# Four column tiles of 32 output rows for each TensorE matmul but the logits, in a gated mix of infini-attention and GEGLU

## The chip, the cores and the metric

The kernel runs on one core of a Trainium2 chip. The metric is the device time in microseconds, the median over runs. All of TensorE (PE), VectorE (DVE), ScalarE (ACT), GpSimd (POOL) and SyncE (SP, which issues the DMAs) take part; each works through its own instructions in program order, and semaphores tie them together.

## The reference

The input x is 2048 rows of 512 (bf16). Two branches read it, and a gate per row mixes them.

```python
g = sigmoid((x * gate_w).sum(-1))                     # one gate per row
out = g * a(x) + (1 - g) * b(x)

# b: GEGLU, inner width 1792
b = (gelu_tanh(x @ w_gate) * (x @ w_up)) @ w_down

# a: 32 heads of 16; the rows in N = 4 segments of L = 512
phi = lambda t: where(t > 0, t + 1, exp(t))
gb = sigmoid(beta)                                    # one number per head
for s in range(4):
    qs, ks, vs = ...                                  # of this segment, per head
    a_dot = softmax(qs @ ks.T / 4 + causal) @ vs
    a_mem = (phi(qs) @ M) / (phi(qs) @ z + 1e-6)      # memory of the segments before
    outs.append(gb * a_mem + (1 - gb) * a_dot)
    M += phi(ks).T @ vs                               # 16 x 16 per head
    z += phi(ks).sum(rows)
a = concat(outs) @ wo
```

## The kernel before, in words

**Layout.** x is kept transposed in `xT`, features on the 128 partitions: four chunks `fc` of 128 features, 2048 columns of rows. Heads come in four chunks `c` of eight (8 x 16 = 128 partitions); in a chunk the heads lie in four pairs `j` of 32 partitions, an even head (`e` = 0) and an odd one. `pr` is a pair of chunks. A segment's 512 rows are four tiles `kt` (or `qt`) of 128.

**Three forms of matmul.** A TensorE matmul takes a stationary operand (loaded ahead by its own instruction, LDWEIGHTS) and streams the columns of a moving one.
- Full: stationary 128 x 128, output on 128 partitions. So work the projections q and k, gate and up (`mm_x`, L320; the first segment's k at L406), v (L422), down (`down`, L834) and output projection (`proj_o`, L839), the memory's denominators (L780) and numerators (L810), the memory update M (L739), and the small ones at the start: `warm` (L371), the transposes of x (L391) and `bps` (L506).
- Row tiles: the logits (`logit_slot`, L574). Four heads at a time, each on its own 16 or 32 partitions of contraction, `tile_position=(32*j, 0)`, each with 128 output partitions.
- Column tiles: softmax times v (`pv_group`, L626) and the gate rows (`gate_rows`, L441). Four matmuls with a stationary operand of 128 x 32, `tile_position=(0, 32*j)`, each writing its own 32 output partitions.

**Memory.** For each pair of chunks of a segment, phi(k) is made by ACT (exp), DVE and POOL (L690 to L701), transposed by DMA (L730), and multiplied with v: `m_update` runs, for each of two chunks and four tiles `kt`, one full matmul with 8 x 17 = 136 moving columns (16 values and a one per head, `VW` = 17). Of its 128 x 136 result only the blocks in which key head and value head agree are wanted. DVE adds the result to `Macc` (L752, L754), and multiplies the value columns with a block mask that also holds the factor of beta (`bdeb`) into `Mbd` (L761), and the ones' columns with a mask into `zbd` (L764). The next segment reads `Mbd` and `zbd`.

**Softmax.** A slot (20 per segment, five per chunk) holds four heads' logits in two PSUM tiles of 128 x 1024; ACT takes the exponential of each (L597), POOL masks it (L606), then come the pv groups, one for the even and one for the odd heads of a chunk. DVE transposes their result (L644), divides it, adds the memory's share and transposes it back into `xT` (L654 to L670), whose columns are free by then.

**PSUM.** The logits, gate pairs and some output tiles share three tiles of two banks (ring `lg`); everything else shares two of one bank (ring `gen`).

**Order.** Each piece of work is a named task; the string `ORDER` (L31 to L102) lists them all by hand, and `Sched.run` emits them in that order, engine by engine. In it PE's small groups (logits `lg`, `pv`, memory) alternate with full ones (`up`, `dn`, `q`, `k`, `v`), about one or two of these between two logit slots. The gates and a part of `up` come first, in the first 75 us; attention runs from there to 250 us; the last segments' down and output projections end the kernel.

The first lines that the change touches, in `mm_x`:

```python
for fc in range(FC):
    nc.tensor.matmul(t, lhsT=W[:, fc, c0:c0 + P], rhs=xT[:, fc, s * L:(s + 1) * L],
                     start=(fc == 0), stop=(fc == FC - 1))
```

Of the kernel before, what the change touches and what calls it, by code (L numbers as in the profile page):

```python
# [23 lines left out]
NCH = H // 8  # L24
HS = DFF // P
# [4 lines left out]
MM = 216  # L30
# [119 lines left out]
def kernel(  # L150
# [39 lines left out]
    def ctile(name, shape, dtype=BF):  # L190
        return cp.tile(shape, dtype, name=name, tag=name)
# [30 lines left out]
    zbd = ctile("zbd", [P, NCH * (P + 2)])  # L222
    bdeb = ctile("bdeb", [P, NCH, 8, DH])
    Mbd = ctile("Mbd", [P, NCH, 8, DH])
    Macc = ctile("Macc", [P, NCH, 8, VW], F32)
    G2 = ctile("G2", [P, NSEG, QB], F32)
    omz = ctile("omz", [P, NSEG, KT], F32)
    omg = ctile("omg", [P, NCH], F32)
# [77 lines left out]
    def evac(engs, g, box, fn, kind="copy", deps=(), alloc=(), frees=(), ring="gen"):  # L306
        return add("e" + g.name, engs, lambda e: fn(e, box["t"]), kind=kind,
                   deps=[g] + list(deps), alloc=alloc, frees=[(ring, g)] + list(frees))

    QK = {}  # L310
    EVQK = {}
    first_ev = {}
# [4 lines left out]

    def mm_x(t, W, c0, s):
        for fc in range(FC):
            nc.tensor.matmul(t, lhsT=W[:, fc, c0:c0 + P], rhs=xT[:, fc, s * L:(s + 1) * L],  # L320
                             start=(fc == 0), stop=(fc == FC - 1))

    def kfree(s, pr):
        k = first_ev[("k", s, pr)]
# [39 lines left out]
    def first_k():  # L364

        tl = {}

        def f_warm(_):
            t = lgtile("warm")
            for i in range(NWARM):  # L370
                nc.tensor.matmul(t[:, 0, :], lhsT=warm[:, 0:P], rhs=warm,  # L371
                                 start=True, stop=True)
# [13 lines left out]
        xe = []  # L386
        prev = op
        for fc in range(FC):
            def f_t(_, fc=fc):
                for kt in range(KT):  # L390
                    nc.tensor.matmul(tl["x", fc][:, kt * P:(kt + 1) * P],  # L391
                                     lhsT=xn[:, kt, fc * P:(fc + 1) * P], rhs=ident,
                                     start=True, stop=True)
            prev = add(f"xt{fc}", "PE", f_t, cost=416, deps=[prev, a_xn])
            xe.append(add(f"ext{fc}", "ACT" if fc % 2 else "DVE",
                          lambda e, fc=fc: copy(e, xT[:, fc, 0:L], tl["x", fc]), kind="copy",
                          deps=[prev], frees=[(("lg", 0), op) if fc < 2
                                              else (("gen", fc - 2), op)]))
        a_x[0] = xe[-1]
        TAB["wdn"] = add("wdn", "SP", lambda _: load_w(nc.sync, wdn, B_w_down), deps=[prev],  # L400
                         kind="wdn")
        last = None
        for fc in range(FC):
            def fn(_, fc=fc):
                for c in range(NCH):
                    nc.tensor.matmul(tl["k", c // 2][:, c % 2, :],  # L406
                                     lhsT=wk[:, fc, c * P:(c + 1) * P], rhs=xT[:, fc, 0:L],
                                     start=(fc == 0), stop=(fc == FC - 1))
            last = add(f"k0f{fc}", "PE", fn, cost=4 * MM, deps=[last, xe[fc], a_wk])
            read_x[0].append(last)  # L410
        for c in range(NCH):
            first_ev[("k", 0, c // 2)] = op
            EVQK[("k", 0, c)] = add(f"ek0.{c}", ["DVE", "ACT"],
                                    lambda e, c=c: copy(e, QK[("k", 0, c // 2)][:, c % 2, :],
                                                        tl["k", c // 2][:, c % 2, :]),
                                    kind="copy", deps=[last], frees=[(("lg", 1 + c // 2), op)])
            odd_copy(0, c, EVQK[("k", 0, c)])

    def v_group(s, kt, engs):
        def mms(t):  # L420
            for fc in range(FC):
                nc.tensor.matmul(t[:, :], lhsT=xT[:, fc, s * L + kt * P:s * L + (kt + 1) * P],  # L422
                                 rhs=wv[:, fc, :], start=(fc == 0), stop=(fc == FC - 1))
# [12 lines left out]
    def gate_rows():  # L436

        def mms(t):
            for fc in range(FC):
                for s in range(NSEG):  # L440
# [4 lines left out]
        g, box = group("", "gz", 4 * MM, mms, a_x + [TAB["gwB"]], mode="col")  # L445
        tl = {}

        def f_tt(e, t):
# [54 lines left out]
    TAB["gwB"] = add("gwB", "DVE", f_gwB, kind="gwB", deps=[a_gw])  # L503

    def f_bps(t):
        nc.tensor.matmul(t[:, 0:NCH], lhsT=hot8[:, :, :].rearrange("p a b -> p (a b)"),  # L506
                         rhs=beta8[:, :], start=True, stop=True)

    def f_omg(e):
        nc.vector.tensor_scalar(out=omg[:, :], in0=tb[:, :], scalar1=-0.5, scalar2=0.5,  # L510
# [104 lines left out]
    def pv_group(s, c, e):  # L615
# [19 lines left out]
            deps.append(PVT[s][-1])  # L635
        def mk():
            TT[(s, c)] = rtile("T", [P, 2, QB, 32], F32)
        g, box = group(f"{s}.{c}{'eo'[e]}", "pv", 546, mms, deps, mode="col", also=("T", mk) if e == 0 else None,
                       frees=[("pT", XT_[(g0 + w, h)]) for w in slots for h in range(2)])
        PVT[s].append(g)  # L640
        key = (s, c)
# [92 lines left out]
    def m_update(s, pr):  # L734
        def mms(t):
            for i in range(2):
                c = 2 * pr + i
                for kt in range(KT):
                    nc.tensor.matmul(t[:, i * 8 * VW:(i + 1) * 8 * VW],  # L739
                                     lhsT=PKt[(s, pr)][:, i, kt, :],  # L740
                                     rhs=vz[s % 2][:, kt, 8 * c * VW:8 * (c + 1) * VW],
                                     start=(kt == 0), stop=(kt == KT - 1))
        g, box = group(f"{s}.{pr}", "M", 8 * 66, mms,
                       [PKD[(s, pr)]] + [EVV[(s, kt)] for kt in range(KT)]
                       + ([TAB[("mbd", s - 1)], TAB[("zbd", s - 1)]] if s else []),
                       frees=[("pk", PKD[(s, pr)])])
# [2 lines left out]
        def f_acc(e, t):  # L749
            dst = Macc[:, 2 * pr:2 * pr + 2, :, :].rearrange("p c h w -> p (c h w)")  # L750
            if s == 0:
                nc.vector.tensor_copy(dst, t[:, 0:16 * VW])  # L752
            else:
                nc.vector.tensor_add(dst, t[:, 0:16 * VW], dst)  # L754
        acc = evac("DVE", g, box, f_acc, kind="acc")
        TAB[("acc", s, pr)] = acc
        if pr == 0:
            return

        def f_mbd(_):  # L760
            nc.vector.tensor_mul(Mbd[:, :, :, :], Macc[:, :, :, 0:DH], bdeb[:, :, :, :])  # L761

        def f_zbd(_):
            nc.vector.tensor_mul(  # L764
                zbd[:, :].rearrange("p (c n) -> p c n", c=NCH)[:, :, 0:P]
                .rearrange("p c (j m) -> p c j m", j=4)[:, :, :, 0:2],
                Macc[:, :, :, DH].rearrange("p c (j e) -> p c j e", j=4),
                bd[:, :, 0].rearrange("p (j e) -> p j e", j=4)[:, None, :, :]
                .to_broadcast((P, NCH, 4, 2)))
        deps = [TAB[("acc", s, 0)], acc, t_eb] + [TAB[("num", s, c)] for c in range(NCH) if s]  # L770
# [4 lines left out]
    def mem_den(s):  # L775
        bx = {}

        def mms(t):
            for c in range(NCH):
                nc.tensor.matmul(t[:, :], lhsT=zbd[:, c * P:(c + 1) * P],  # L780
                                 rhs=PQ[(s, c // 2)][:, c % 2, :],
                                 start=(c == 0), stop=(c == NCH - 1))
# [24 lines left out]

    def mem_num(s, c):
        def mms(t):
            nc.tensor.matmul(t[:, :], lhsT=Mbd[:, c, :, :].rearrange("p h d -> p (h d)"),  # L810
                             rhs=PQ[(s, c // 2)][:, c % 2, :], start=True, stop=True)
# [19 lines left out]

    def down(t, s, qt, lo, hi, stop):
        for hs in range(lo, hi):
            nc.tensor.matmul(t[:, :], lhsT=G[:, s, hs, qt * P:(qt + 1) * P], rhs=wdn[:, hs, :],  # L834
                             start=(hs == 0), stop=stop and (hs == HS - 1))

    def proj_o(t, s, qt, cs, first):
        for c in cs:
            nc.tensor.matmul(t, lhsT=xT[:, c, s * L + qt * P:s * L + (qt + 1) * P],  # L839
                             rhs=wo[:, c, :], start=first and c == 0, stop=(c == NCH - 1))  # L840

    def store(s, qt, osb):
        q0 = s * L + qt * P
# [112 lines left out]
```

## Time and profile before

| | |
|---|---|
| time, median of 3 runs | 283.71 us (283.68 to 283.9) |
| the profiled execution's own time | 283.82 us |
| its span in the profile | 282.1 us |
| PE busy | 271.1 us, 96%, 2280 matmuls recorded |
| weight loads (PEld) | 118.4 us, 2320 recorded |
| ACT busy | 204.2 us, 72% |
| DVE busy | 174.6 us, 62% |
| POOL busy | 125.9 us, 45% |
| granted PE clock | full in all 40 slices |
| code loads (q8) | 18 of 16 KB |

The span runs from the first to the last instruction in the profile; the execution's own time holds the start and the end around it. Shares are of the span. A matmul's record is longer than the time until the next one may start, since matmuls overlap: a full one of 512 columns shows 380 ns, and the next starts 216 ns later. So what a matmul costs PE is read from start to start, and a busy PE need not stream. A few matmul records are missing from the trace (2280 of 2320).

### The profile page before, as it was taken

The numbers are of one execution on the slowest core, as the hardware profiler recorded it, in microseconds if no ns is written. First come the engines' busy times: TensorE is split into PE (matmuls) and PEld (weight loads), VectorE is DVE, ScalarE is ACT, GpSimd is POOL, SyncE is SP. The second block draws the span as 40 slices with busy tenths as digits, with TensorE's granted clock in tenths as the row PEclk, the third lists the DMA queues.
The fourth block names the chain that finished last, engine by engine and source line by source line (L and its number), as shares of the span: only waits on it lengthen the run. The fifth ranks groups of instructions, "written<-read, shape, count | busy, mean of one in ns | idle before, by whom it ended". The sixth has DMA issues, their size and how long they took to land.

```text
span 282.1 us, 5660 instructions
## 1 busy us (share of the span) xinstructions
PE 271.1 (96%) x2280; PEld 118.4 (42%) x2320; DVE 174.6 (62%) x324; ACT 204.2 (72%) x223; POOL 125.9 (45%) x220
## 2 busy tenths in 40 slices
PE   8999999999999999999899999999999999999994
PEld 4444444444444443444334444433444444344441
DVE  2100002510787878999969659989698877857721
ACT  3555654326689989999999999999999999950000
POOL 8000000060066686495575858584547657650000
PEclk9999999999999999999999999999999999999999
DMA  7973970000002211100001101000002000000011
GB/s 233 347 129 75 344 251 2 0 0 2 1 19 46 15 30 28 21 0 2 2 0 21 37 3 38 2 21 1 2 0 58 21 19 21 2 21 0 21 56 57
DMA packets 22019, 13.74 MB, mean 49 GB/s; under 512 B 14056, under 2 KB 20968, under 8 KB 21992
## 3 DMA queue, kind: packets, MB, share of 16 engines
q1 hardware_dynamic: 21448, 12.85, 16.8%
q10 hardware_dynamic: 544, 0.52, 0.5%
q8 instruction: 18, 0.29, 0.4%
q14 instruction: 9, 0.07, 0.1%
HBM read 8.13 MB, written 2.10 MB: 36 GB/s over the span
## 4 chain that ended last, share of the span: by engine, by line
PE 86%; DVE 8%; POOL 2%; issue 2%; DMA 1%; ACT 1%; SPq 0%; POOLq 0%
PE dn L834 18%; PE gt L320 17%; PE up L320 16%; PE lg L574 8%; PE pv L626 6%; PE dn L839 5%; PE q L320 4%; PE v L422 3%; PE k L320 3%; POOL pkT L701 2%; PE k L406 1%; PE M L739 1%; PE warm L371 1%; DMA pk<-pkT 1%; DVE T L644 1%
## 5 line engine op out<-in xcount | busy, mean ns | idle before, releaser
L597 ACT ACTIVATE pT<-lg 128x1024 bf16<-128x1024 f32 x160 | 153.4, 1032 | 8.2 <-PE lg L574 6.3
L606 POOL TENSOR_SCALAR_AFFINE_SELECT pT<-pT 128x512 bf16<-128x512 bf16 (+1 forms) x160 | 89.6, 588 | 54.7 <-ACT pT L597 52.4
L497 DVE TENSOR_TENSOR G<-up,G 128x512 bf16<-128x512 f32 x56 | 37.9, 683 | 52.5 <-PE up L320 49.2
L320 PE MATMUL up<-xT,wup 128*128 128x512 bf16 x211 | 54.0, 380 | 1.1 <-DVE G L497 0.5
L834 PE MATMUL dn<-wdn,G 128*128 128x512 bf16 x217 | 52.5, 380 | 0.5
L320 PE MATMUL gt<-xT,wga 128*128 128x512 bf16 x219 | 50.4, 379 | 0.3
L487 ACT ACTIVATE G<-gt 128x1024 bf16<-128x1024 f32 x28 | 27.7, 1023 | 31.1 <-PE gt L320 31.1
L320 PEld LDWEIGHTS <-wga 128*128 128x128 bf16 x224 | 21.8, 98 | 26.4 <-issue 0.4
L834 PEld LDWEIGHTS <-G 128*128 128x128 bf16 x224 | 20.6, 98 | 24.7 <-issue 2.4
L320 PEld LDWEIGHTS <-wup 128*128 128x128 bf16 x224 | 19.8, 97 | 25.6 <-issue 5.6
L458 POOL COPY G<-tt 32x16 f32<-32x16 f32 x16 | 3.2, 197 | 49.1 <-DVE tt L450 48.5
L644 DVE STREAM_TRANSPOSE T<-pv 128x512 f32<-128x512 f32 x32 | 22.5, 707 | 2.4 <-PE pv L626 2.3
L626 PE MATMUL pv<-pT,vz 128*32 128x256 bf16 (+2 forms) x640 | 23.2, 275 | 0.6 <-DVE osb L881 0.2
L881 DVE TENSOR_SCALAR osb<-dn,omz 128x512 bf16<-128x512 f32 x14 | 10.5, 750 | 19.6 <-PE dn L839 16.7
L701 POOL TENSOR_TENSOR pkT<-E,Q 128x1024 bf16<-128x1024 bf16 x6 | 12.8, 2128 | 21.1 <-PE q L320 18.6
L879 ACT ACTIVATE osb<-dn,omz 128x512 bf16<-128x512 f32 x2 | 1.4, 688 | 26.3 <-PE dn L839 26.3
L574 PE MATMUL lg<-qT,kT 16*128 16x256 bf16 (+2 forms) x320 | 17.9, 273 | 0.4
L574 PE MATMUL lg<-qT,kO 32*128 32x128 bf16 (+2 forms) x320 | 17.9, 272 | 0.0
L626 PEld LDWEIGHTS <-vz 128*32 128x32 bf16 x640 | 12.6, 96 | 11.1 <-issue 2.3
L320 PE MATMUL q<-xT,wq 128*128 128x512 bf16 x58 | 15.8, 380 | 1.0 <-DVE T L644 0.7
L839 PE MATMUL dn<-wo,xT 128*128 128x512 bf16 x62 | 15.7, 380 | 0.0
L422 PE MATMUL v<-wv,xT 128*128 128x512 bf16 x61 | 15.3, 379 | 0.2
(88 smaller groups left out, 244.7 us busy)
## 6 DMA issues: line engine op xcount, KB each, us to landing
out_dram<-osb SPq DMA_DIRECT2D x16, 128.0 KB, 1.7
wup<-in_B_w_up_dram SPq DMA_DIRECT2D x1, 1792.0 KB, 8.1
wdn<-in_B_w_down_dram SPq DMA_DIRECT2D x1, 1792.0 KB, 13.6
wga<-in_B_w_gate_dram SPq DMA_DIRECT2D x1, 1280.0 KB, 10.7
wq<-in_A_wq_dram SPq DMA_DIRECT2D x1, 512.0 KB, 6.1
wga<-in_B_w_gate_dram SPq DMA_DIRECT2D x1, 512.0 KB
wv<-in_A_wv_dram SPq DMA_DIRECT2D x1, 512.0 KB, 8.0
wo<-in_A_wo_dram SPq DMA_DIRECT2D x1, 512.0 KB, 9.1
```

The source lines that it names most:

```text
L320: nc.tensor.matmul(t, lhsT=W[:, fc, c0:c0 + P], rhs=xT[:, fc, s * L:(s + 1) * L], start=(fc == 0), stop=(fc == FC - 1))
L422: nc.tensor.matmul(t[:, :], lhsT=xT[:, fc, s * L + kt * P:s * L + (kt + 1) * P], rhs=wv[:, fc, :], start=(fc == 0), stop=(fc == FC - 1))
L487: ge = evac("ACT", g, box, lambda e, t: nc.scalar.activation(dst, t[:, :, :], AF.Gelu_apprx_tanh), kind="gelu", ring="lg")
L497: UPT[(s, hs)] = evac("DVE", g, box, lambda e, t: nc.vector.tensor_mul(G[:, s, hs, :], t[:, :], G[:, s, hs, :]), kind="up")
L574: nc.tensor.matmul(A[j // 2][:, j % 2, at * P:(at + nq) * P], lhsT=l, rhs=r, start=True, stop=True, tile_position=(32 * j, 0))
L597: nc.scalar.activation(pT[(s, t, h)][:, :, :], A[h][:, :, :], AF.Exp, scale=0.25)
L606: nc.gpsimd.affine_select(out=v, in_=v, pattern=pat, compare_op=ALU.is_ge, fill=0.0, base=0, channel_multiplier=-1)
L626: nc.tensor.matmul(t[32 * j:32 * j + 32, qb * P:(qb + nq) * P], lhsT=vz[s % 2][:, kt, h * VW:h * VW + 32], rhs=pT[(s, t0 + w, j // 2)][:, ...
L644: nc.vector.transpose(TT[key][:, e, :, :].rearrange("p a b -> p (a b)"), t[:, :])
L701: nc.gpsimd.tensor_add(d[:, :, :], box["E"][:, :, :], box["Q"][:, :, :])
L834: nc.tensor.matmul(t[:, :], lhsT=G[:, s, hs, qt * P:(qt + 1) * P], rhs=wdn[:, hs, :], start=(hs == 0), stop=stop and (hs == HS - 1))
L839: nc.tensor.matmul(t, lhsT=xT[:, c, s * L + qt * P:s * L + (qt + 1) * P], rhs=wo[:, c, :], start=first and c == 0, stop=(c == NCH - 1))
```

## The change

A helper issues four matmuls of 32 output partitions for each full one, with the same moving operand and a quarter of the stationary one each. All full matmuls go through it but M, which is written out: there each of the four tiles multiplies its 32 partitions of keys (two heads) with the value columns of these two heads alone, 2 x 17 = 34. So `Macc` holds two heads' columns per partition where it held eight, and `Mbd` and `zbd` are made from it by a broadcast over the four tiles; `Mbd` takes four DVE instructions, one per chunk, instead of one. The logits stay row tiles. The tasks' `mode` labels go too; nothing reads them. The string `ORDER` is the same in both files, and each engine has its tasks in the same sequence.

```diff
-    Macc = ctile("Macc", [P, NCH, 8, VW], F32)
+    Macc = ctile("Macc", [P, NCH, 2, VW], F32)
...
+    def mm4(out, lhsT, rhs, start, stop):
+
+        for j in range(4):
+            a = slice(32 * j, 32 * j + 32)
+            nc.tensor.matmul(out[a], lhsT=lhsT[:, a], rhs=rhs, start=start, stop=stop,
+                             tile_position=(0, 32 * j), skip_group_check=True)
...
         for fc in range(FC):
-            nc.tensor.matmul(t, lhsT=W[:, fc, c0:c0 + P], rhs=xT[:, fc, s * L:(s + 1) * L],
-                             start=(fc == 0), stop=(fc == FC - 1))
+            mm4(t, W[:, fc, c0:c0 + P], xT[:, fc, s * L:(s + 1) * L], fc == 0, fc == FC - 1)
...
-                    nc.tensor.matmul(t[:, i * 8 * VW:(i + 1) * 8 * VW],
-                                     lhsT=PKt[(s, pr)][:, i, kt, :],
-                                     rhs=vz[s % 2][:, kt, 8 * c * VW:8 * (c + 1) * VW],
-                                     start=(kt == 0), stop=(kt == KT - 1))
+                    for j in range(4):
+                        h = 8 * c + 2 * j
+                        a = slice(32 * j, 32 * j + 32)
+                        nc.tensor.matmul(t[a, i * 2 * VW:(i + 1) * 2 * VW],
+                                         lhsT=PKt[(s, pr)][:, i, kt, a],
+                                         rhs=vz[s % 2][:, kt, h * VW:(h + 2) * VW],
+                                         start=(kt == 0), stop=(kt == KT - 1),
+                                         tile_position=(0, 32 * j), skip_group_check=True)
...
-                nc.vector.tensor_add(dst, t[:, 0:16 * VW], dst)
+                nc.vector.tensor_add(dst, t[:, 0:4 * VW], dst)
...
-            nc.vector.tensor_mul(Mbd[:, :, :, :], Macc[:, :, :, 0:DH], bdeb[:, :, :, :])
+            for c in range(NCH):
+                nc.vector.tensor_mul(
+                    Mbd[:, c, :, :].rearrange("p (j e) d -> p j e d", j=4),
+                    Macc[:, c, :, 0:DH][:, None, :, :].to_broadcast((P, 4, 2, DH)),
+                    bdeb[:, c, :, :].rearrange("p (j e) d -> p j e d", j=4))
...
-            nc.tensor.matmul(t[:, :], lhsT=G[:, s, hs, qt * P:(qt + 1) * P], rhs=wdn[:, hs, :],
-                             start=(hs == 0), stop=stop and (hs == HS - 1))
+            mm4(t, G[:, s, hs, qt * P:(qt + 1) * P], wdn[:, hs, :], hs == 0,
+                stop and (hs == HS - 1))
```

In the same way `mm4` takes the place of the full matmul in `first_k`, `v_group`, `f_bps`, `mem_den`, `mem_num` and `proj_o`.

More of the change, by code (lines that the diff above doesn't have):

```diff
@@ L370, in f_warm @@
             for i in range(NWARM):
-                nc.tensor.matmul(t[:, 0, :], lhsT=warm[:, 0:P], rhs=warm,
-                                 start=True, stop=True)
+                mm4(t[:, 0, :], warm[:, 0:P], warm, True, True)
         w = add("warm", "PE", f_warm, cost=427 * NWARM, alloc=["lg"])
@@ L390, in f_t @@
                 for kt in range(KT):
-                    nc.tensor.matmul(tl["x", fc][:, kt * P:(kt + 1) * P],
-                                     lhsT=xn[:, kt, fc * P:(fc + 1) * P], rhs=ident,
-                                     start=True, stop=True)
+                    mm4(tl["x", fc][:, kt * P:(kt + 1) * P], xn[:, kt, fc * P:(fc + 1) * P],
+                        ident, True, True)
             prev = add(f"xt{fc}", "PE", f_t, cost=416, deps=[prev, a_xn])
@@ L405, in fn @@
                 for c in range(NCH):
-                    nc.tensor.matmul(tl["k", c // 2][:, c % 2, :],
-                                     lhsT=wk[:, fc, c * P:(c + 1) * P], rhs=xT[:, fc, 0:L],
-                                     start=(fc == 0), stop=(fc == FC - 1))
+                    mm4(tl["k", c // 2][:, c % 2, :], wk[:, fc, c * P:(c + 1) * P],
+                        xT[:, fc, 0:L], fc == 0, fc == FC - 1)
             last = add(f"k0f{fc}", "PE", fn, cost=4 * MM, deps=[last, xe[fc], a_wk])
@@ L421, in mms @@
             for fc in range(FC):
-                nc.tensor.matmul(t[:, :], lhsT=xT[:, fc, s * L + kt * P:s * L + (kt + 1) * P],
-                                 rhs=wv[:, fc, :], start=(fc == 0), stop=(fc == FC - 1))
+                mm4(t, xT[:, fc, s * L + kt * P:s * L + (kt + 1) * P], wv[:, fc, :], fc == 0,
+                    fc == FC - 1)
         g, box = group(f"{s}.{kt}", "v", 4 * MM, mms,
@@ L444, in mms @@
                                      skip_group_check=True)
-        g, box = group("", "gz", 4 * MM, mms, a_x + [TAB["gwB"]], mode="col")
+        g, box = group("", "gz", 4 * MM, mms, a_x + [TAB["gwB"]])
         tl = {}
@@ L505, in f_bps @@
     def f_bps(t):
-        nc.tensor.matmul(t[:, 0:NCH], lhsT=hot8[:, :, :].rearrange("p a b -> p (a b)"),
-                         rhs=beta8[:, :], start=True, stop=True)
+        mm4(t[:, 0:NCH], hot8[:, :, :].rearrange("p a b -> p (a b)"), beta8[:, :], True, True)
     def f_omg(e):
@@ L637, in mk @@
             TT[(s, c)] = rtile("T", [P, 2, QB, 32], F32)
-        g, box = group(f"{s}.{c}{'eo'[e]}", "pv", 546, mms, deps, mode="col", also=("T", mk) if e == 0 else None,
+        g, box = group(f"{s}.{c}{'eo'[e]}", "pv", 546, mms, deps, also=("T", mk) if e == 0 else None,
                        frees=[("pT", XT_[(g0 + w, h)]) for w in slots for h in range(2)])
@@ L738, in mms @@
                 for kt in range(KT):
-                    nc.tensor.matmul(t[:, i * 8 * VW:(i + 1) * 8 * VW],
-                                     lhsT=PKt[(s, pr)][:, i, kt, :],
-                                     rhs=vz[s % 2][:, kt, 8 * c * VW:8 * (c + 1) * VW],
-                                     start=(kt == 0), stop=(kt == KT - 1))
-        g, box = group(f"{s}.{pr}", "M", 8 * 66, mms,
+                    for j in range(4):
[6 more added lines that the diff above has]
+                                         tile_position=(0, 32 * j), skip_group_check=True)
+        g, box = group(f"{s}.{pr}", "M", 8 * 30, mms,
                        [PKD[(s, pr)]] + [EVV[(s, kt)] for kt in range(KT)]
@@ L751, in f_acc @@
             if s == 0:
-                nc.vector.tensor_copy(dst, t[:, 0:16 * VW])
+                nc.vector.tensor_copy(dst, t[:, 0:4 * VW])
             else:
-                nc.vector.tensor_add(dst, t[:, 0:16 * VW], dst)
+                nc.vector.tensor_add(dst, t[:, 0:4 * VW], dst)
         acc = evac("DVE", g, box, f_acc, kind="acc")
@@ L766, in f_zbd @@
                 .rearrange("p c (j m) -> p c j m", j=4)[:, :, :, 0:2],
-                Macc[:, :, :, DH].rearrange("p c (j e) -> p c j e", j=4),
+                Macc[:, :, :, DH][:, :, None, :].to_broadcast((P, NCH, 4, 2)),
                 bd[:, :, 0].rearrange("p (j e) -> p j e", j=4)[:, None, :, :]
@@ L779, in mms @@
             for c in range(NCH):
-                nc.tensor.matmul(t[:, :], lhsT=zbd[:, c * P:(c + 1) * P],
-                                 rhs=PQ[(s, c // 2)][:, c % 2, :],
-                                 start=(c == 0), stop=(c == NCH - 1))
+                mm4(t, zbd[:, c * P:(c + 1) * P], PQ[(s, c // 2)][:, c % 2, :], c == 0,
+                    c == NCH - 1)
         g, box = group(f"{s}", "den", 4 * MM, mms,
@@ L809, in mms @@
         def mms(t):
-            nc.tensor.matmul(t[:, :], lhsT=Mbd[:, c, :, :].rearrange("p h d -> p (h d)"),
-                             rhs=PQ[(s, c // 2)][:, c % 2, :], start=True, stop=True)
+            mm4(t, Mbd[:, c, :, :].rearrange("p h d -> p (h d)"),
+                PQ[(s, c // 2)][:, c % 2, :], True, True)
         bx = {}
@@ L833, in down @@
         for hs in range(lo, hi):
-            nc.tensor.matmul(t[:, :], lhsT=G[:, s, hs, qt * P:(qt + 1) * P], rhs=wdn[:, hs, :],
-                             start=(hs == 0), stop=stop and (hs == HS - 1))
+            mm4(t, G[:, s, hs, qt * P:(qt + 1) * P], wdn[:, hs, :], hs == 0,
+                stop and (hs == HS - 1))
     def proj_o(t, s, qt, cs, first):
         for c in cs:
-            nc.tensor.matmul(t, lhsT=xT[:, c, s * L + qt * P:s * L + (qt + 1) * P],
-                             rhs=wo[:, c, :], start=first and c == 0, stop=(c == NCH - 1))
+            mm4(t, xT[:, c, s * L + qt * P:s * L + (qt + 1) * P], wo[:, c, :],
+                first and c == 0, c == NCH - 1)
     def store(s, qt, osb):
```

## The prediction, made before the changed kernel ran

> **What bounds the kernel now.** I read the engine totals first, then busy time by stage, then the chain of waits, and last the starts of single instructions around the places that the change touches.
>
> ```profile
> PE 271.1 (96%) x2280; PEld 118.4 (42%) x2320; DVE 174.6 (62%) x324; ACT 204.2 (72%) x223; POOL 125.9 (45%) x220
> PE dn L834 18%; PE gt L320 17%; PE up L320 16%; PE lg L574 8%; PE pv L626 6%; PE dn L839 5%; PE q L320 4%; PE v L422 3%; PE k L320 3%; POOL pkT L701 2%; PE k L406 1%; PE M L739 1%; PE warm L371 1%; DMA pk<-pkT 1%; DVE T L644 1%
> 85.00:250.00 165.00, 159.85 (x1727) 68.34 (x1756) 135.85 (x250) 157.10 (x171) 107.34 (x163) 1.00 0.08 17
> ```
>
> The first line is the whole span of 282.1 us, the second the chain that ended last (PE holds 86% of it), the third the attention stage alone (PE, weight loads, DVE, ACT, POOL, clock 1.00). PE sets the end. But in the attention stage ACT is busy 157.1 of 165 us, so a faster PE soon meets ACT there.
>
> A busy PE is not yet a useful PE. The timeline shows where it loses:
>
> ```profile
> 53.32 0.59 PE L320 MATMUL gt<-xT,wga 128*128 128x512 bf16 x2
> 53.85 1.05 PE L441 MATMUL gz<-xT,gwB 128*32 128x512 bf16 x16
> 54.83 0.39 PE L320 MATMUL gt<-xT,wga 128*128 128x512 bf16 x1
> ```
> ```profile
> 199.80 0.38 PE L839 MATMUL dn<-wo,xT 128*128 128x512 bf16 x1
> 200.12 0.40 PE L574 MATMUL lg<-qT,kT 16*128 16x256 bf16 x12
> 200.44 1.31 PE L626 MATMUL pv<-pT,vz 128*32 128x512 bf16 x40
> ```
> ```profile
> L739 PE MATMUL M<-vz,pk 128*128 128x136 bf16 x48 | 3.9, 223 | 0.2 <-DVE G L497 0.2
> ```
>
> Columns of the first two fences: start us, us, engine, line. Full matmuls (128*128) of 512 columns start 216 ns apart, median of 480 neighbours on L320. From the last full one to a logit matmul it is 311 ns (199.80 to 200.12), to a column-tiled one 309, from the last pv matmul (128 columns, 56 ns pitch) to a full one 151. So each change among the three forms of matmul, full, row tiles (lg) and column tiles (pv, gz), costs 93 to 101 ns in which no column streams. In gz, 16 column tiles make four quads: they start at 53.847, 54.074, 54.290 and 54.505 us, so a quad of 512 columns also takes 216 ns, with its four members started within 11 ns.
>
> **The change, part by part.**
>
> *Changes of form.* Program order has 194 of them: full to row 69, row to full 61, col to full 21, full to col 13, row to col 19, col to row 11. With all but the logits column-tiled, only row and col remain: 80 and 80. The 34 between full and col go. Leaving pv for a full matmul takes 161 ns from the first member of its last quad where the pitch is 56: 21 x 105 = 2.2 us. Entering takes 309 for 216: 13 x 93 = 1.2 us. Sum 3.4 us gained, 33 of the 34 on a PE that is the chain. The other 160 keep their price: row to col is 144 ns, row to full 147.
>
> *The stagger.* Where a single matmul ended a stretch before lg, a quad now does, and its last member starts 10 ns late (gz: 54.505 to 54.515, then 312 to the next form). 68 such places: 0.7 us lost.
>
> *Steady quads.* 952 full matmuls of 512 columns become quads; gz's pitch of 216 ns says: nothing. (gz's first pitch is 227, but a full matmul's first pitch after a change is 226 too.) Yet gz's members read four different stretches of xT, and the new quads read one rhs four times, which no row shows. Bounds: 215 ns (gz's shortest pitch) to 227 (its longest), 952 times -1 to +11 ns: -1.0 to +10.5 us. I take 216, as gz is nearest, and keep the upper end as a rival.
>
> *Weight loads.* 2320 become 5392, of 32 columns each. They start 3 to 4 ns apart and run 96 ns beside the quad before. pv's quads of 128 columns keep a 56 ns pitch with four loads each, so under 216 ns they are hidden; the cover would be gone if four loads took over 216 ns. [...]
>
> *Memory update M.* 48 full matmuls of 136 columns, 59 ns apart, become 48 quads of 34 columns. Between 25 ns (34 columns at 216/512 ns each, and the 11 ns stagger) and 59 (no gain): 0 to 1.6 us; a loss would need quads slower than pv's 56 with four times the columns. I take the middle, 42 ns: 0.8 us gained.
>
> *DVE.* Macc reads 68 columns where 272 took 435 ns; rows of 128x128 f32 take 215, so about 220 x 6 = 1.3 us less. Mbd (993 ns) becomes four of 128x128, 250 each by L800: the same. DVE has 29 us free in the stage: no term. No engine but PE and these DVE rows changes its sequence, and ORDER is letter for letter the same, so nothing is moved past a queue. Waits written in PE's program: 492 before, 490 after.
>
> *Issue.* The unseen cost: PE's program grows from 4642 to 10786 instructions, 8 in 216 ns, 27 ns each. The trace bounds the sequencer. Its last record stands at 274.04 us, when 16 loads and 17 matmuls have not started: it runs 33 instructions ahead. (At L506 it is 32 ahead.) At 200.11 us 99 instructions start within 1.32 us, so 66 were issued in 1.32 us: at most 20 ns each. 27 is slower than that, so steady quads do not starve. The lead in time falls from 3.5 to 0.9 us; the one wait of the sequencer itself, 51 ns at L506, stays hidden. Cost between 0 and the 4.1 us of the rival below; I take 0, because those 1.32 us, the densest of the trace, show no gap that issue would have to explain. [...]
>
> *Code loading.* 18 loads of 16 KB in the trace, 0.9 to 1.5 us each, become about 42. One covers 256 instructions, 6.9 us of steady quads: hidden, unless one takes over some 4 us.
>
> PE's sum: 3.4 + 0.8 - 0.7 = 3.5 us. What is late next is ACT:
>
> ```profile
> L597 ACT ACTIVATE pT<-lg 128x1024 bf16<-128x1024 f32 x160 | 153.4, 1032 | 8.2 <-PE lg L574 6.3
> ```
>
> ACT waited 6.3 us for logits, and that is what PE can give it. In about 30 of the 165 us (135 to 144, 186 to 193, 198 to 211) its exponentials already follow each other without a gap, and PE waits for their buffers; there the gain is lost: 3.5 x 30/165 = 0.6. That leaves 2.9 us. The profiled execution took 283.82 us (span 282.1 and 1.7 around it), 0.11 over the median of 283.71: 283.82 - 2.9 = 280.9, as a median 280.8.
>
> **The rivals.**
>
> *Issue limits the dense stretches (slower).* Place: pv, M and the logits in three parts. At 20 ns per instruction a pv group (40) needs 0.80 us and has 0.53, M (64) 1.28 for 0.34, such a logit slot (24) 0.48 for 0.41 with its changes of form: 32 x 0.27 + 6 x 0.94 + 32 x 0.07 = 16.5 us short. The 475 quads of the stage give back 56 ns each, 27 us, and the lead bridges 0.66 us at a time; how much stays unbridged no row says. A quarter is 4.1 us: 283.7 - 2.9 + 4.1 = 284.9. At 18 ns the same sum is 11.7 us short, a quarter of it 2.9: from there on it decides. For it: the bound of 20 is near. Against: 99 instructions without a sign of it.
>
> *Reading one rhs four times slows the quads (slower).* Each ns on the pitch costs 0.95 us, so 3 ns decide; at 220 it is 283.7 - 2.9 + 3.8 = 284.6, at gz's longest 227 it is 291.3. For it: no row shows such reading. Against: pv and gz read four streams at full pace.
>
> *ACT and DVE take half.* In 15 places of the stage PE already stands over 0.15 us beyond the price of a change of form, 5.1 us in all, waiting for their buffers or inputs. If half of the gain ends in these waits, 1.7 us are left: 282.0. For it: ACT 157.1 of 165. Against: its 7.9 us free are twice the gain.
>
> *It does not do what it says.* The new order is not there, and if leaving pv still empties the array, only stagger and M remain: about 283.7 + 0.7 = 284.4. Against: from the last quad of one pv group to the next group it is 82 ns with a wait in it (200.946 to 201.028 us), not 161.
>
> **How the numbers follow.** Forecast 0.57; issue 0.14 (0.12 slower, 0.02 same); four reads 0.10 (0.09 and 0.01); half 0.14 (0.12 faster, 0.02 same); not as said 0.05, slower. Faster 0.69, same 0.05, slower 0.26; 0.2% (0.57 us) is about what a measurement of this kernel can tell from no change. The forecast's own range: all of it with M at 25 ns, 3.4 + 1.6 - 0.7 = 4.3, so 279.4; up to 282.0. The range goes on to 285.5, over the rivals at 284.4 to 284.9. Beyond it lie issue at 20 ns with more than a quarter unbridged (0.05), a pitch over 221 (0.06) and, below, 0.02: 0.13.
>
> **What would show it.** Right: full-sized groups as 128*32 quads 216 ns apart; 56 ns, not 161, from pv's last quad to the next col group; M quads at 25 to 59; ACT's wait for lg down from 6.3 us towards 4; PE's span shorter mostly between 85 and 250 us. Wrong: PE gaps right after pv or M with no releaser (issue); a quad pitch of 219 or more everywhere, the first 75 us longer too (reads); gaps before lg released by ACT (half).

## The result, and the profile after

| | before | changed |
|---|---|---|
| time, median | 283.78 us (283.68 to 283.9, 4 runs) | 285.31 us (285.19 to 285.54, 4 runs) |
| profiled execution, its span | 283.82 us, 282.1 us | 285.54 us, 283.7 us |

The ratio is 1.0055, 95% interval [1.0037, 1.0072]: slower by 1.5 us, where 2.9 us of gain were forecast. The profile of one experiment below (e11) was taken at a granted clock of 0.851, so only its time is used.

First the page of the changed kernel: engine totals, the chain by engine and by line, the code loads' queue (loads, MB, share), and two groups (busy us, mean ns | idle us before them and what ended it).

```profile
PE 271.2 (96%) x5392; PEld 132.4 (47%) x5392; DVE 174.5 (61%) x333; ACT 203.6 (72%) x223; POOL 124.5 (44%) x220
...
q8 instruction: 42, 0.69, 1.0%
...
PE 76%; DVE 13%; DMA 5%; SPq 3%; issue 1%; ACT 1%; POOL 0%
...
L599 ACT ACTIVATE pT<-lg 128x1024 bf16<-128x1024 f32 x160 | 152.7, 1032 | 9.4 <-PE lg L576 8.4
```

PE's share of the chain fell from 86 to 76%; DVE's rose from 8 to 13%, the DMAs' from 1 to 5%. So PE waits for more than it did, and for others than ACT: ACT's own wait for logits grew from 6.3 to 8.4 us. In the attention stage every engine has a little less done by 250 us:

```profile
85.00:250.00 165.00, 159.27 (x3312) 73.87 (x3305) 134.84 (x257) 156.03 (x170) 106.87 (x164) 1.00 0.09 19
```

To see where PE loses, both traces were laid side by side, group of matmuls by group. Each gap between starts is split into a price without any wait (columns / 2.4 + 2.5 ns, a line through the two measured pitches, 216 ns for 512 columns and 56 for 128; 95 ns for a change of form, measured at 93 to 101 before, and 10 more where a quad is left, as in gz) and the rest, the waits:

| stage | price, us | waits, us | sum |
|---|---|---|---|
| first, to 75 us | -0.20 | +1.39 | +1.2 |
| attention | -4.59 | +4.96 | +0.4 |
| end | 0.00 | 0.00 | 0.0 |

(For M's quads the formula gives 17 ns where 25 are measured; 0.4 us of the waits is that.)

The price did fall. It was given back in waits, at three kinds of places.

**The first stage.** PE's timeline of the changed kernel (start us, us, engine, line; in brackets the idle time before, and its releaser), then that of the kernel before:

```profile
15.83 2.34 PE L314 MATMUL gt<-xT,wga 128*32 128x512 bf16 x40
18.80 3.50 PE L314 MATMUL gt<-xT,wga 128*32 128x512 bf16 x56 [0.63 <-DMA xT<-in_A_x_dram]
```
```profile
15.55 5.34 PE L320 MATMUL gt<-xT,wga 128*128 128x512 bf16 x24
```

Where 24 gt matmuls ran without a break, PE now stands twice, for 0.79 us before 18.80 and for 0.29 before 19.31, until transposes of x have landed. Code loads do it, as e10 and e12 show below without a quad. The changed kernel has them at 9.55, 16.53 and 20.97 us, each 1.0 to 1.2 us long; the kernel before has one before 45 us, at 17.87. Packets of the transposes hung beside the load at 16.53: 26 that started at 17.01 to 17.10 us took 1.42 to 1.46 us and ended at 18.46 to 18.52, 0.8 us after the load's end at 17.70. (28 others, started at 13.56 to 14.09 us with no load under way, took 1.5 to 2.1 us: a load is not all that can hold them up.)

**Mbd.** The DVE group of before, then of the changed kernel, and what PE waited for (us in total, times, longest):

```profile
L761 DVE TENSOR_TENSOR Mbd<-Macc,bdeb 128x512 bf16<-128x512 f32 x3 | 3.0, 993 | 0.0
```
```profile
L768 DVE TENSOR_TENSOR Mbd<-Macc,bdeb 128x128 bf16<-128x128 f32 x12 | 5.1, 485 | 0.0
```
```profile
PE up L320 <- DVE G L497: 0.5, 1, 0.5
```
```profile
PE up L314 <- DVE G L500: 1.3, 3, 0.8
...
PE pv L628 <- DVE G L500: 0.5, 1, 0.5
```

A quarter of Mbd takes 485 ns on the mean, not 250: four of the twelve take 279 to 281 ns, the other eight 429 to 720. What parts them is POOL. Each of the eight starts while POOL masks the softmax (`pT`, L608) and ends 140 to 142 ns after the end of that mask. Of the four, three start with no mask under way and one 1 ns after a mask's start. In the first group the quarters start at 99.62, 99.82, 100.47 and 101.10 us and end at 99.90, 100.54, 101.18 and 101.59; masks end at 100.40, 101.04 and 101.44. So a quarter waits for the mask under way, POOL begins its next mask before the next quarter starts, and that one waits again. The single instruction of before waited once per group: each of its three ends 541 to 542 ns after the end of the mask that it started in. (This is read from the traces; no run moved the masks.)

The three groups of four last 1.96, 1.45 and 1.71 us, where the single instruction took 1.05, 0.86 and 1.07. The timeline shows POOL's masks, and who waits in the end: DVE's next copies out of `up`'s PSUM start late, and PE's next `up` waits for that buffer.

```profile
99.62 2.24 POOL L608 TENSOR_SCALAR_AFFINE_SELECT pT<-pT 128x512 bf16<-128x512 bf16 x4 [2.04 <-ACT pT L599]
99.62 1.96 DVE L768 TENSOR_TENSOR Mbd<-Macc,bdeb 128x128 bf16<-128x128 f32 x4
101.07 0.40 PE L576 MATMUL lg<-qT,kO 32*128 32x256 bf16 x12
...
101.51 1.28 DVE L500 TENSOR_TENSOR G<-up,G 128x512 bf16<-128x512 f32 x2
102.24 1.05 PE L314 MATMUL up<-xT,wup 128*32 128x512 bf16 x16 [0.77 <-DVE G L500]
```

**After M.** M's quads start 25 ns apart, and in five of its six groups the eight take 178 to 191 ns from first to last start, where they took 411 to 425. But the work behind M starts no earlier: from the first M to it, the five took 623, 517, 559, 522 and 524 ns before and take 622, 530, 615, 540 and 545 now. It needs the PSUM buffer that DVE is still copying out of, as the timeline of the changed kernel shows at one of the five places (there `vz<-v`):

```profile
210.58 0.69 DVE L177 CAST vz<-v 128x512 bf16<-128x512 f32 x1
...
210.78 0.38 PE L744 MATMUL M<-vz,pk 128*32 128x34 bf16 x32
...
211.33 1.26 PE L314 MATMUL dn<-wdn,G 128*32 128x512 bf16 x20 [0.17 <-DVE vz L177]
```

### The profile page after: what moved, and what is told of

Same layout as the page of the kernel before. It is cut to its first block, busy times and chain, and to the rows that moved or that the text cites. A ratio compares the mean times of both kernels' runs of the same rounds, so it can differ in the third digit from the quotient of the medians.

```text
span 283.7 us, 11855 instructions
## 1 busy us (share of the span) xinstructions
PE 271.2 (96%) x5392; PEld 132.4 (47%) x5392; DVE 174.5 (61%) x333; ACT 203.6 (72%) x223; POOL 124.5 (44%) x220
## 4 chain that ended last, share of the span: by engine, by line
PE 76%; DVE 13%; DMA 5%; SPq 3%; issue 1%; ACT 1%; POOL 0%
PE dn L314 23%; PE gt L314 15%; PE up L314 15%; PE lg L576 7%; PE pv L628 5%; PE v L314 5%; PE q L314 3%; SPq L234 3%; PE k L314 3%; DVE G L500 2%; DMA xT<-in_A_x_dram 2%; DVE T L646 2%; DMA wdn<-in_A_x_dram 1%; DMA pk<-pkT 1%; DVE Mbd L768 1%
## 5 line engine op out<-in xcount | busy, mean ns | idle before, releaser
L608 POOL TENSOR_SCALAR_AFFINE_SELECT pT<-pT 128x512 bf16<-128x512 bf16 (+1 forms) x160 | 87.7, 576 | 56.3 <-ACT pT L599 53.9
L314 PE MATMUL up<-xT,wup 128*32 128x512 bf16 x896 | 55.7, 380 | 1.6 <-DVE G L500 1.3
L314 PE MATMUL dn<-wdn,G 128*32 128x512 bf16 x896 | 53.3, 380 | 0.7 <-DVE T L646 0.2
L314 PE MATMUL gt<-xT,wga 128*32 128x512 bf16 x896 | 51.2, 379 | 0.7 <-DMA xT<-in_A_x_dram 0.6
L314 PEld LDWEIGHTS <-wga 128*32 128x32 bf16 x896 | 25.6, 97 | 23.6 <-issue 1.3
L314 PEld LDWEIGHTS <-G 128*32 128x32 bf16 x896 | 24.1, 96 | 21.9 <-issue 3.0
L314 PEld LDWEIGHTS <-wup 128*32 128x32 bf16 x896 | 22.9, 96 | 23.4 <-issue 5.8
L314 PEld LDWEIGHTS <-xT 128*32 128x32 bf16 x512 | 13.7, 96 | 13.3 <-issue 2.0
L314 PE MATMUL q<-xT,wq 128*32 128x512 bf16 x256 | 16.4, 380 | 0.8 <-DVE T L646 0.8
L314 PE MATMUL k<-xT,wk 128*32 128x512 bf16 x256 | 16.0, 380 | 0.9 <-DVE T L646 0.6
```

The costliest lines, as they stand in the source:

```text
L314: nc.tensor.matmul(out[a], lhsT=lhsT[:, a], rhs=rhs, start=start, stop=stop, tile_position=(0, 32 * j), skip_group_check=True)
L608: nc.gpsimd.affine_select(out=v, in_=v, pattern=pat, compare_op=ALU.is_ge, fill=0.0, base=0, channel_multiplier=-1)
```

## The experiments

Two theories were set against each other. Mine: quads cost nothing in themselves, and three neighbours take the gain: the code loads (by their number), Mbd (by its four instructions), and DVE's copy that the work behind M waits for. The rival: dense programs of small instructions slow PE or its sequencer, wherever they stand. Each run is timed beside the kernel before, whose median was then 283.72 to 283.86 us. The switch that several of them use:

```diff
 def mm4(out, lhsT, rhs, start, stop):
+    if not S.quads:
+        nc.tensor.matmul(out, lhsT=lhsT, rhs=rhs, start=start, stop=stop)
+        return
     for j in range(4):
```

**r1: the changed kernel again.** No edit.

> The changed kernel once more, for a second trace of it. Theory A (code loads): the early loss belongs to the kernel. In its first trace PE has lost 1.4 us against the kernel before by 20 us, at three waits (for x at 4.6 us, for a k at 6.3, for a transposed x at 18.8), while 16 KB code loads run at 9.5, 16.5 and 21.0 us where the kernel before has one, at 17.9. Then the waits come back, 1.0 to 1.7 us by 25 us. Rival (chance): the transfers of that one execution started late; then the early loss is under 0.5 us in this trace, and the time of 285.3 would have to be made elsewhere. Time either way 285.3 (285.1 to 285.6).

285.29 us, ratio 1.0049 [1.0036, 1.0063]. The first stage lost 0.92 us again, with code loads at 9.84, 16.35 and 20.43 us. It is no accident of one run.

**e1: quads only after the first stage** (`S.quads` is false until the task "opened", at about 75 us).

> The changed kernel, but with full matmuls up to the point where attention opens (about 75 us), quads after it; M, Macc and Mbd as changed. Theory A (quads in the first stage pull two more code loads into the time of the x transposes): the early loss of about 1.2 us goes, and only one code load lies before 25 us: 284.1 (283.8 to 284.4). Rival (the loss is all in the attention stage: M, Mbd and the stagger): 285.2, unchanged within 0.2.

284.70 us, 1.0033 [1.0021, 1.0044]. The first stage is back (waits +0.15 us, one code load before 25 us, at 17.82), the attention stage kept its loss of 0.54. I had expected 284.1: the place was right, but 0.6 us came back where I had expected 1.2. It also answers a rival that I had not named, that x's transposes came late because they were issued late. The changed kernel issues the first at 4.95 us (4.28 before) and it lands at 16.29 (14.71 before); e1 issues it at 4.88, and it lands at 14.76.

**e2: the kernel before with quads in the first stage alone** (`S.quads` is true until "opened"; M, Macc and Mbd as before).

> The kernel before, but with quads in the first stage alone, up to the point where attention opens; everything after it, M and Mbd too, is as before. Theory A: 1.2 us slower than the kernel before, 284.9 (284.5 to 285.3), with code loads near 9.5, 16.5 and 21 us and a wait of PE near 18.8 us that ends with a transfer of x. Rival (nothing is lost in the first stage): 283.6, or 0.2 less for the two changes of form around the gate rows.

284.97 us, 1.0035 [1.0023, 1.0047]. By 19 us 1.10 us are lost, 0.2 come back at gz, and the attention stage is unchanged. PE in its first 30 us waits for x twice:

```profile
PE gt L319 <- DMA xT<-in_A_x_dram: 0.4, 2, 0.2
```

e1 and e2 split the loss by stage, but both move quads and code loads together. Three runs without a quad part them: the kernel before, its seven warm-up matmuls (on zeros, at 1 to 4 us) cut into more and narrower ones of the same total length. That adds instructions ahead of everything else and moves the code loads.

**e10, e11, e12: code loads moved, no quads.**

```diff
-            for i in range(NWARM):                                    # 7
-                nc.tensor.matmul(t[:, 0, :], lhsT=warm[:, 0:P], rhs=warm,
+            for i in range(45):                                       # e11: 14 of 256, e12: 21 of 170
+                nc.tensor.matmul(t[:, 0, 0:80], lhsT=warm[:, 0:P], rhs=warm[:, 0:80],
```

> The kernel before, no quads, but its 7 warm-up matmuls of 512 columns are 45 of 80 columns (the same stream, 76 instructions more): so its first code load, at 17.9 us, should come at about 9.5 us, as the changed kernel's first does, and the next at about 38 instead of 46. Theory (a code load holds up the transposes of x that are under way, and what the kernel loses in the first stage depends on where loads fall among them): the four landings between 18.5 and 23 us come about 1 us earlier than in the kernel before, whose load stood among them; no PE wait in the first 30 us, time 283.8 +- 0.3 (the landings were not waited for). Rival (it is the number of PE instructions, or the quads themselves, that slow the first stage): landings as before.

> The kernel before, no quads, but its 7 warm-up matmuls of 512 columns are 14 of 256 (14 instructions more): its first code load should come at about 16.4 us instead of 17.9, close to the changed kernel's second. Theory (code loads hold up the transposes of x): PE's gt at 17.5 to 19 us waits for xT by 0.2 to 0.8 us, with a DMA as the releaser, in a kernel without one quad in it; part of it comes back at gz, which waits for DVE: time 284.1 (283.8 to 284.6). Rival (the quads slow the first stage, not the loads): no PE wait there, 283.8 +- 0.2. If there is no wait although the load came at 16.4, one load alone is not enough and it takes the two, at 9.5 and 16.5 us.

> The kernel before, no quads, with its 7 warm-up matmuls of 512 columns as 21 of 170 columns (28 instructions more): its first code load should come at about 14.9 us instead of 17.9. With the 7 as 45 of 80 columns the load came at 13.8 us and took 1.9, and gt waited 0.2 us for xT before 18.1. Theory (a load that falls between about 13.5 and 16 us holds up the last transposes of x's second segment, which gt needs at 17.9): a PE wait of 0.1 to 0.8 us for xT at 17.9 to 18.8 us with a DMA as the releaser, time 284.2 +- 0.3. Rival (that run's wait came from the length of its load, or from its 0.15 us later start): no wait, 283.8 +- 0.2.

e10 took 284.16 us, 1.0021 [1.001, 1.0032], e12 284.22, 1.0018 [1.0002, 1.0034], e11 283.82, 1.0002 [0.9993, 1.0011]. PE's timelines of e10 and then of e12:

```profile
18.11 3.43 PE L320 MATMUL gt<-xT,wga 128*128 128x512 bf16 x14 [0.21 <-DMA xT<-in_A_x_dram]
```
```profile
18.52 2.97 PE L320 MATMUL gt<-xT,wga 128*128 128x512 bf16 x12 [0.29 <-DMA xT<-in_A_x_dram]
```

The wait of the changed kernel, in kernels without one quad: so the code loads do it, not the quads. My places for the loads were off: e10's came at 13.85 us (and took 1.94), not 9.5; e12's at 16.40 (1.11 us), not 14.9. The load at 17.87, before the change, cost PE nothing: in its first 30 us PE has no wait for x there. e10 did not land its later transposes earlier, as I had expected. e11's expected wait did not show in its time; where its load fell in the timed runs is not known. By the medians one load cost about 0.4 us (by the intervals 0.1 to 1.0); that the changed kernel's 1.2 us are its three loads together was not tried by itself.

**e4: the kernel before with Mbd in four instructions.**

```diff
-            nc.vector.tensor_mul(Mbd[:, :, :, :], Macc[:, :, :, 0:DH], bdeb[:, :, :, :])
+            for c in range(NCH):
+                nc.vector.tensor_mul(Mbd[:, c, :, :], Macc[:, c, :, 0:DH], bdeb[:, c, :, :])
```

> The kernel before, with one edit: Mbd is made in four DVE instructions, one per chunk, instead of one. Theory C (the four instructions hold up DVE's copies out of PSUM, and PE behind them): Mbd takes 1.4 to 1.9 us where it took 1.0, PE waits 0.5 to 0.75 us longer behind at least two of the three: 284.6 (284.1 to 284.9). Rival (the waits come from quads in M alone): 283.75 within 0.2.

285.22 us, 1.0052 [1.0039, 1.0066], more than I expected: waits +1.32 us in attention, 0.85 of it before `up` at 101.1 us and 0.55 before pv at 177.8. PE still runs full matmuls here, so this edit on DVE alone costs nearly as much as the whole change. Here too the eight longer quarters of twelve end 141 to 143 ns after a mask of POOL. Its DVE group and PE's waits:

```profile
L762 DVE TENSOR_TENSOR Mbd<-Macc,bdeb 128x128 bf16<-128x128 f32 x12 | 5.1, 480 | 0.0
```
```profile
PE up L320 <- DVE G L497: 1.3, 2, 0.9
...
PE pv L626 <- DVE G L497: 0.5, 1, 0.5
```

**e6: the changed kernel with Mbd in two instructions**, one for the even and one for the odd heads of all chunks.

> The changed kernel with Mbd in two DVE instructions of 256 columns (one for the even, one for the odd heads) instead of four of 128. Theory C: the pair takes 0.9 to 1.2 us instead of 1.4 to 1.9, and the two waits of PE behind it (0.75 and 0.55 us) mostly go: 284.4 (284.1 to 284.8). Rival (the wait is the buffers' and not Mbd's): 285.3 within 0.2.

284.15 us, 1.0011 [1.0002, 1.0019]: 1.2 us under the changed kernel. By the traces 0.9 of it lie in the attention stage; the rest lies in the first stage, whose loss differs between executions (0.7 us here, 1.2 and 0.92 in the changed kernel's two). The pairs take 1.19, 1.11 and 1.57 us, the last more than I expected. The DVE group and wait; the wait for pv is gone:

```profile
L768 DVE TENSOR_TENSOR Mbd<-Macc,bdeb 128x256 bf16<-128x256 f32 x6 | 3.9, 684 | 0.0
```
```profile
PE up L314 <- DVE G L500: 0.5, 2, 0.4
```

**e5: M's quads issued twice** (128 instructions per group where the changed kernel has 64; the second pass writes over the first).

```diff
-                for kt in range(KT):
+                for kt in list(range(KT)) * 2:
```

> The changed kernel with M's eight quads issued twice in each of the six groups, the second time over the first (the result is the same): 0.2 us more of matmuls in each, 1.2 us in all. Theory D (the work after M waits for DVE's copy out of the PSUM buffer that was filled before M, so M's own length is hidden): 285.3, unchanged within 0.2, and the wait after M shrinks from 0.25-0.33 us to 0.05-0.13. Rival (M is on the path): 286.3.

285.67 us, 1.0059 [1.0043, 1.0075], span 283.9 against 283.7. The median is 0.36 us over the changed kernel's, more than the 0.2 that I allowed, but the two intervals overlap almost wholly, and the rival's 286.3 lies 0.6 higher still. M's sixteen quads take 450 ns instead of 189, and the work behind M starts 624, 531, 611, 538 and 543 ns after the first M, within 5 ns of the changed kernel. So M's length is worth nothing there, in either direction. The run also settles issue. In the changed kernel's trace PE's sequencer is 44 instructions ahead (its record at 277.99 us, when 20 loads and 24 matmuls have not started; 33 before the change). With that lead, 84 of the 128 were issued within these 450 ns, an estimated 5.4 ns each at most on the mean.

**e3: the changed kernel with M, Macc and Mbd as before** (`m_update` is that of the kernel before).

> The changed kernel, but M as 48 full matmuls of 136 columns, Macc with eight heads, and Mbd in one instruction, all as before. In the changed kernel's trace M's eight quads take 0.2 us where it was 0.47, but PE then waits 0.25 to 0.33 us for DVE's copy out of the other PSUM buffer; and Mbd's four instructions take 1.4 to 1.9 us where one took 1.0, with waits of 0.75 and 0.55 us of PE behind them. Theory B (the whole M part loses): M gives back 1.2 us of matmuls and adds about 0.1 us for each of up to 6 changes of form, its waits of 1.5 us go, Mbd's 1.3 go: 284.2 (283.9 to 284.6). Rival (these waits only move, ACT sets the pace): 285.3, unchanged within 0.2. Rival (M's gain was real): 286.2.

283.89 us, 1.0001 [0.9992, 1.001]. Undoing the memory part alone brings the time back to that of before: attention now gains 0.9 us (price -1.98, waits +1.07), and the first stage loses as much.

**e7: both undone,** quads only after the first stage, M, Macc and Mbd as before.

> Quads only where attention runs (from about 75 us on), and M, Macc and Mbd as before: the first two losses left out. By the traces the first stage then costs 0.1 us more than before and attention gains 0.9: 282.9 (282.6 to 283.3), faster than the kernel before. Rival (each removal only opens the next wait, ACT sets the pace): 283.7, no faster than before.

283.32 us, 0.9983 [0.9975, 0.9992]: faster than before. The price is 1.98 us lower, 1.2 of it go into many small waits for DVE's copies and ACT. What is left to save in it is the stagger: 79 places where a quad stands ahead of logits, 11 before the change.

**e9: quads only where they save a change of form.**

```diff
+        quad = {n for r in runs for n in r if n.startswith("pv")}      # runs: PE's tasks between two logit slots
+        for _ in runs:                                                # group: a whole down + output accumulation
+            quad |= {group(n) for r in runs if any(group(m) in quad for m in r)
+                     for n in r if not n.startswith("M")}
+        form = {n: group(n) in quad for r in runs for n in r}
```

> The kernel before, with quads only where they save changes of form: full matmuls become quads in those stretches between two logit slots that hold pv (and, for down and output projection, in the rest of the same accumulation). The first stage, M, Macc and Mbd stay as before. 3268 matmuls, 164 changes of form (before 194, quads everywhere in attention 169), and 27 more places than before where a col-tiled matmul stands ahead of logits (quads everywhere: 68 more). Theory (a quad costs nothing but the late start of its last member ahead of logits, and saves the changes): against the run with quads everywhere in attention and M as before (283.3 us), 41 staggers of 10 ns and 5 changes of 95 ns less, 0.9 us, of which about a third ends in DVE's and ACT's waits as there: 282.7 (282.3 to 283.1), code loads before 25 us one, first stage as before. Rival (the waits for DVE and ACT take all that PE gives beyond the 0.5 us of that run): 283.3 +- 0.2.

282.14 us, 0.9945 [0.9934, 0.9957]: 1.6 us faster than the kernel before, 3.2 than the changed one, and below my range. Changes of form 164 (e7: 169), col-tiled matmuls ahead of logits 38 (79); price -2.78 us, waits +1.15. The waits did not grow with the gain, so the rival falls. Page and windows of e9:

```profile
q8 instruction: 25, 0.41, 0.6%
...
PE 88%; DVE 9%; issue 1%; ACT 0%
...
L616 ACT ACTIVATE pT<-lg 128x1024 bf16<-128x1024 f32 x160 | 152.7, 1033 | 7.5 <-PE lg L593 6.2
```
```profile
85.00:250.00 165.00, 160.33 (x2331) 72.88 (x2356) 136.89 (x251) 157.47 (x172) 107.87 (x165) 1.00 0.07 18
```

PE holds 88% of the chain again, and ACT does more by 250 us (157.47 us) than in the kernel before (157.10) or the changed one (156.03).

## Why the prediction was wrong, step by step

The time lies in the range, but the sign was missed; none of the four rivals was the cause. That the range holds the time is luck: it was opened upwards for rivals that did not come true.

- **Steady quads, right.** 216 ns on the median of 818 pitches, the four members within 25 ns; the rival of reading one rhs four times falls.
- **Changes of form, right in kind, a little too large.** From pv's last quad to the next column group 56 ns, not 161, at ten places, and 60 to 120 at seven more (1.5 us in all); entering 216, not 309 (0.93 us); at gz 0.2. So 2.6 of the 3.4 us can be read. The rest stands at places where PE waits for something else.
- **Stagger, right:** 0.6 us for 0.7. From a quad's first member to the logits it is 321 ns on the median, where it was 312 from a full matmul, at 69 places.
- **Issue, right at 0.** An estimated 5.4 ns per instruction at most (e5), not the bound of 20. The rival falls.
- **M, the wrong step of the sum on PE.** The pitch is 25 ns, better than the 42 I took. But I put the 0.8 us on the path, and they are not on it: DVE's copy ends later than M in either form (e5). I had asked what ends PE's waits as a whole, not what ends the wait behind M; the starts behind M (92 to 212 ns after its last matmul, whose price is 59) were within reach in the trace of before. M's quads keep their pitch of 25 ns with four weight loads each. The formula above makes an estimated 17 ns of their 34 columns, so at most 8 ns are left for the loads.
- **Code loading, the step that failed first.** "Hidden, unless one takes over some 4 us": I asked only whether PE runs out of instructions. It does not: 24 more loads came for 6144 more instructions, 256 each as I took, and the longest took 1.94 us (e10). No run tried the 4 us, an estimate of mine. But a load is a DMA (queue q8, 16 KB), and it holds up the transposes that PE needs: 1.2 us in the first stage, 0.4 us for one load alone (e10, e12).
- **DVE, the step that failed most.** "Four of 128x128, 250 each: the same", and "29 us free in the stage: no term". They took 485 ns on the mean, and the free 29 us were not beside Mbd: there the copies out of `up` queue behind it, and PE behind those. It cost 1.3 us (e4), and with two instructions the time came down by 1.2, 0.9 of it in attention (e6). The price of 250 came from a row (L800) whose three instructions take 245 to 255 ns and were held up by nothing. The row that was nearest, Mbd itself, showed the wait that was missing: all three ended 541 to 542 ns after a mask of POOL. Eight instructions of Mbd's form that start under no mask (`Nm`, L823, before) take 683 ns on the median, and four quarters without a wait an estimated 281 + 3 x 202 = 887 ns (their starts lie 202 ns apart): 0.2 us more per group, 0.6 in all. The groups grew by 0.92, 0.59 and 0.64 us, 2.15 in all. The other 1.5 are waits for masks: what the instructions take beyond 281 or 683 ns is 2.45 us now and was 0.93. So of the 2.15 an estimated 0.6 are the price of four instructions for one, and the larger part is POOL's.
- **ACT, mis-sized.** I let ACT take 0.6 us and its wait for logits fall to 4 us; it rose to 8.4, since PE came later. Once the other losses are undone, what DVE and ACT take is 1.15 to 1.2 us (e7, e9), between the 0.6 of the forecast and the half of the rival.

In sum: 2.6 us of changes of form less 0.6 of stagger leave 2.0 gained, where the forecast had 2.7. M gives nothing. Mbd takes 1.3 and the first stage's waits 1.4. That makes a loss of 0.7; the other 0.8 of the 1.5 us lost is spread over many small waits that no run here took apart.

## What to carry to other kernels

An edit that makes an engine's program longer should be priced at the DMAs too: look for the stretch where the path waits closely behind transfers, and ask what a code load does to them (here 42 loads for 18, and 1.2 us in the first stage). An operation split into smaller ones is priced by what is queued behind it at that moment, not by the free time of its engine over a stage; and if one instruction already ends a fixed time after a neighbour's, each piece can wait for that neighbour anew, as eight of the twelve quarters did. And a form that pays only where it meets its like belongs only there: quads in the stretches around pv alone (e9) beat both kernels by more than everywhere.

## What the runs showed that was not expected

- A 16 KB code load took 0.9 to 1.9 us. Packets of the transposes, started in its time, hung until about 0.8 us after its end (10 of them at the load at 17.87 us before the change, 26 at the one at 16.53 after it).
- A DVE instruction for Mbd that started during a mask of POOL ended a fixed time after that mask: 140 to 142 ns for 128 columns (changed kernel), 274 to 276 for 256 (e6), 541 to 542 for 512 (before). In the changed kernel one of 128 columns took 279 ns without such a wait and up to 720 with it. (One that started 1 ns after a mask did not wait: 281 ns.)
- Issue on PE: an estimated 5.4 ns per instruction at most on the mean (e5, from 84 instructions in 450 ns), with 44 instructions of lead.
- A column-tiled quad of 34 columns started every 25 ns (30 on the mean in e5, 450 ns over 15 steps), four weight loads each included.
